# When the early weight conversions run in a fused retention, max-MLP and gated-MLP kernel

## The chip, the cores and the metric

The kernel runs on one core of one Trainium2 chip. The metric is the device time of one launch in microseconds (us). Three runs of the kernel before gave 906.43, 902.74 and 906.63 us; the median is 906.43 us.

## The reference

Three layers follow one another. The input has 4 sequences of 576 tokens, 8 heads of 64, so 2304 tokens of 512 features.

```python
scores = (1 / sqrt(64)) * q @ k.T                      # per batch and head
ret = (scores * D) @ v                                  # D[i, j] = gamma_h ** (i - j) for i >= j, else 0
x = ret as (2304, 512)
h = maximum(maximum(x @ w1, x @ w2), x @ w3)            # 512 -> 768   "first layer"
x = h @ w_out                                           # 768 -> 512   "second layer"
g = x @ w_gate; val = x @ w_val                         # 512 -> 1536  "third layer"
out = (g * sigmoid(g) * val) @ w_out2                   # 1536 -> 512
```

The weights arrive as 64-bit floats, seen by the kernel as pairs of 32-bit words.

## The kernel before, in words

**Precision.** Every product of matrices is made in three matmuls of a high and a low part (`xh`, `xl`, `wh`, `wl`). Each matmul has 288 columns (512 in the last product).

**Conversions and spills.** `conv32` turns one 128x512 tile of 64-bit weights into 32-bit floats: two ScalarE (ACT) instructions at L106 and L107, then three VectorE (DVE) instructions at L108 to L110. The 18 tiles of w1, w2, w3 are converted early and stay on the chip. The other 42 tiles are what this case is about: `spill()` loads one such tile (SP queue, 512 KB), converts it, and stores it to a scratch tensor `wd` in memory (SP queue, L298, 256 KB). The order of the 42 is fixed: six tiles of w_out, then, for each pair `k` = 0 to 5 of third-layer column groups, two of w_gate (`g`), two of w_val (`v`), two of w_out2 (`p`). Three buffers hold tiles that are loaded ahead.

**Stages.** The attention runs as 32 units `n` (a sequence, a half of 288 tokens, a pair of heads). From n = 4 on it is mixed with the first layer: after each unit come slices (`f_slice`, L311), one slice being 12 matmuls into one of two PSUM buffers, taken out by ACT (`hmax`, L315) or by a DVE maximum (L317), and stored to `h_d` after the third. After the last unit come the last 18 slices, mixed with the loads of the second layer's weights (`wo_load`, L377 to L380) and of its first inputs (`h_split`: load `hf` L387, high part `hh` on ACT L390, low part `hl` on POOL or DVE L391). The second layer is eight passes `o` (L470), each with four groups of 18 matmuls (L487), each group taken out by ACT (L492 in the first four passes, L496 in the last four). The inputs of pass `o + 1` are loaded and split during pass `o`. In passes 1 and 3 `x_ops` (L420 to L429) makes the third layer's inputs of the first half with a chain of DVE and ACT work; in passes 4 to 7 the result goes through memory (`x2d`, L502) for the second half. The third layer uses a seven-product scheme in place of eight (`half`, L577), with its weights prepared by `w_ops` (loads of `wd` into `sf` and `s`, DVE sums L456 to L459, ACT high parts L455 to L462, POOL low parts L460 to L465) and `p_ops` (load `of` L521, high part `ph` L523, low part `pl` on POOL L524).

**What sets the order.** TensorE (PE) follows the written order in the attention and in the third layer. Everything else is placed by a list scheduler that models the times of the instructions and issues an instruction as early as its model allows; the program that results is fixed, and each engine and the SP queue then run it strictly in that order, one waiting instruction holding all behind it. `paced` is the hook against too much earliness: the conversion of a spill is not placed before the instructions kept in `pace`. In the attention and the first layer these are the last `hmax` instructions. For the second layer `pace.clear()` (L469) empties it, so that the spills called there (L499) may be placed as early as the model likes.

**Where spills are called before.** One after each unit from n = 9 on (L359, 23 spills), one more where n is 12, 16, 20, 24, 28 (L363, 5), one in each of the six rounds of last slices (L398), one at the end of each of the eight passes of the second layer (L499).

Of the kernel before, what the change touches and what calls it, by code (L numbers as in the profile page):

```python
# [13 lines left out]
ACTF = mybir.ActivationFunctionType  # L14
# [13 lines left out]
NHB = 2 * B  # L28
# [34 lines left out]
def retention_moe(ctx, tc, consts, q, k, v, w1, w2, w3, w_out, w_gate, w_val, w_out2, out):  # L63
    nc = tc.nc
    pe, act, dve, pool, sp = nc.tensor, nc.scalar, nc.vector, nc.gpsimd, nc.sync
# [36 lines left out]
    def conv32(t):  # L102
        u = t.bitcast(U32).rearrange("p (n two) -> p n two", two=2)
        z = stg.tile([P, 512], U32, name="wz", tag="wz", bufs=2)
        l = stg.tile([P, 512], U32, name="wl", tag="wl")
        act.activation(f(z), f(u[:, :, 1]), ACTF.Copy, scale=float(2.0 ** -112))  # L106
        act.activation(l, u[:, :, 0], ACTF.Copy, scale=float(2.0 ** -29))  # L107
        dve.tensor_scalar(z, z, 3, None, ALU.logical_shift_left)  # L108
        dve.scalar_tensor_tensor(z, u[:, :, 1], 0x80000000, z, ALU.bitwise_and, ALU.bitwise_or)
        dve.tensor_tensor(l, z, l, ALU.add)  # L110
        return f(l)
# [16 lines left out]
    def a_load(n):  # L128
        if n >= NU:
            return  # L130
        b, h, pr = units[n]
        c0 = h * C
        u = {}
        for nm, s in (("k", k), ("q", q), ("v", v)):
            if nm == "q" and n >= PT:
                continue
            u[nm] = att.tile([CK, NC, 2, D], F32, name=f"{nm}n", tag=f"{nm}n", bufs=4)
            for e in range(2):
                sp.dma_start(out=u[nm][:, :, e, :],
                             in_=s[b, 2 * pr + e, c0:c0 + C].rearrange("(a p) d -> p a d", p=CK))  # L140
        if n >= PT:
            u["t"] = att.tile([P, 2, C // 32, 32], F32, name="qk", tag="qk", bufs=3)
            for i, s in enumerate((k, q)):
                for e in range(2):
                    for x in range(2):
                        g = 64 * e + 32 * x
                        sp.dma_start(out=u["t"][g:g + 32, i],
                                     in_=s[b, 2 * pr + e, c0:c0 + C, 32 * x:32 * x + 32].rearrange("(a p) d -> p a d", p=32))
        U[n] = u
# [71 lines left out]
    def a_value(n):  # L221
        b, h, pr = units[n]
        u = U.pop(n)
        z = stz[n % 3]
        o = psa.tile([P, C], F32, name="o_ps", tag="o_ps")
        for c in range(NC):
            for e in range(2):
                oc = o[64 * e:64 * e + 64, c * CK:(c + 1) * CK]
                if c or h:
                    pe.matmul(oc, z[:, c, e], u["qg"][:, c], start=c == 1 - h, stop=False, skip_group_check=True)  # L230
        for c in range(NC):
            for e in range(2):
                pe.matmul(o[64 * e:64 * e + 64, c * CK:(c + 1) * CK], u["v"][:, c, e], u["pT"][:, e, c],
                          start=False, stop=True, skip_group_check=True)
        xh, xl = [ffn.tile([P, C], F32R, name=f"x{x}", tag=f"x{x}{pr}", bufs=3) for x in "hl"]
        act.activation(xh, o, ACTF.Copy)
        dve.tensor_tensor(xl, o, f(xh), ALU.subtract)
        xs[(2 * b + h, pr)] = (xh, xl)
# [11 lines left out]
    def win_conv(i):  # L250
        if i >= len(win_units):
            return
        if i not in win_ld:
            win_load(i)
        win_load(i + 1)
        hi = ffn.tile([P, 512], F32R, name="wh", tag=f"wh{i}")
        lo = ffn.tile([P, 512], F32R, name="wlo", tag=f"wlo{i}")
        l = conv32(win_ld.pop(i))
        act.activation(hi, l, ACTF.Copy)
        pool.tensor_tensor(lo, l, f(hi), ALU.subtract)  # L260
        w_in[win_units[i]] = (hi, lo)
# [10 lines left out]
    pace = {}  # L272

    def paced(*names):

        st = ExitStack()
        for nm in names:
            if nm in pace:
                st.enter_context(tc.issue_after(pace[nm]))
        return st  # L280

    def sp_load(i):
        if i < len(sp_units) and i not in sp_ld:
            with paced("sp"):
                sp_ld[i] = load_w(sp_units[i][1])

    def spill():
        i = sp_n[0]
        if i >= len(sp_units):
            return  # L290
        sp_n[0] += 1
        sp_load(i)
        with paced("act", "dve"):
            l = conv32(sp_ld.pop(i))
        sp_load(i + 1)
        sp_load(i + 2)
        wd[sp_units[i][0]] = t = dram.tile([P, 512], F32, name=f"wd{i}", tag=f"wd{i}")
        sp.dma_start(out=t, in_=l)  # L298
# [3 lines left out]
    def f_slice(hb, fi, wi):  # L302
        wh, wl = w_in[(fi, wi)]
        cw = TOK[hb][1]
        ps = ps_mm.tile([P, C], F32, name="ps", tag="mm")[:, 0:cw]
        n = 0
        for kc in range(KD):
            xh, xl = xs[(hb, kc)]
            ksl = slice(kc * P, kc * P + P)
            for l, r in ((wh, xl), (wl, xh), (wh, xh)):  # L310
                pe.matmul(ps, l[:, ksl], r, start=n == 0, stop=n == 3 * KD - 1)  # L311
                n += 1
        if wi == 0:
            mx[hb] = ffn.tile([P, C], F32, name="hmax", tag="hmax", bufs=3)[:, 0:cw]
            pace["act"] = act.activation(mx[hb], ps, ACTF.Copy).ins  # L315
        else:
            pace["dve"] = dve.tensor_tensor(mx[hb], ps, mx[hb], ALU.max).ins  # L317
        if wi == 2:
            pace["sp"] = sp.dma_start(out=h_d[hb][fi], in_=mx[hb]).ins
# [3 lines left out]
    def f_some(n):  # L323
        for _ in range(n):
            if fq:
                f_slice(*fq.pop(0))
# [15 lines left out]
    for n in range(NU):  # L342
        if n % NP == 0 and n:
            fq += [(n // NP - 1, fi, wi) for fi in range(F1) for wi in range(3)]
        a_load(n + 4)
        a_value(n)
        a_state(n + 1)
        a_score(n + 1)
        quota, ncv = ((2, 3) if n >= 9 else (1, 2)), 0
        if 1 <= n < 4:  # L350
            ncv = 1
        elif 4 <= n < 9:
            ncv = 3
        for _ in range(min(ncv, len(win_units) - wc)):
            win_conv(wc)
            wc += 1
        f_some(quota[0])
        if n >= 9:
            spill()  # L359
        a_prep(n + 2)  # L360
        f_some(quota[1])
        if n >= 9 and n % 4 == 0:
            spill()  # L363
    pe_order.__exit__(None, None, None)
    psa_cm.__exit__(None, None, None)
# [29 lines left out]
    for i in range(F1):  # L395
        wo_load(i)
        h_split(0, i)
        spill()  # L398
        f_some(3)
    ffn_cm.__exit__(None, None, None)  # L400


# [11 lines left out]
    def x_tiles(blk):  # L414
        X[blk] = [xp.tile([P, 7, KH, C], F32R, name=f"x{x}", tag=f"xo{x}{blk}") for x in "hl"]
# [54 lines left out]
    for o in range(NHB):  # L470
        hb = order2[o]
        sb, blk, side = hb // 4, hb % 2, (hb // 2) % 2
        if sb == 0:
            if side == 0:
                x_tiles(blk)
                sc = [scratch() for j in range(KH)]
        else:
            st2 = wr.tile([P, 7, C], F32, name="sf", tag="sf")
        for e in (0, 2, 1, 3):
            ps = ps_mm.tile([P, C], F32, name="ps2", tag="mm")  # L480
            n = 0
            for fi in range(F1):
                wh, wl = wo[fi]
                hh, hl = hsp[(o, fi)]
                es = slice(e * P, e * P + P)
                for l, r in ((wh, hl), (wl, hh), (wh, hh)):
                    pe.matmul(ps, l[:, es], r, start=n == 0, stop=n == 3 * F1 - 1)  # L487
                    n += 1
            j, kh = e % KH, e // KH
            if sb == 0:  # L490
                sf, b12 = sc[j]
                act.activation(b12 if side and not kh else sf[:, 2 * side * kh + (1 - side) * kh], ps, ACTF.Copy)  # L492
                if side and kh:
                    x_ops(blk, j, sf, b12)
            else:
                act.activation(st2[:, e], ps, ACTF.Copy)  # L496
            for fi in ((0, 1), (3, 4), (2,), (5,))[e]:
                h_split(o + 1, fi)
        spill()  # L499
        if sb:  # L500
            x2d[hb] = t = dram.tile([P, KD, C], F32, name=f"x2d{hb}", tag=f"x2d{hb}")
            sp.dma_start(out=t, in_=st2[:, 0:KD])  # L502
            if o == NHB - 4:
                w_ops("g", 0)
            elif o == NHB - 3:
                w_ops("v", 0)
# [183 lines left out]
```

## Time and profile before

| quantity | value |
|---|---|
| median of three runs | 906.43 us (902.74 to 906.63) |
| the profiled execution's own time | 902.81 us |
| span of that execution's trace | 901.0 us |
| PE busy | 833.3 us, 92% of the span |
| DVE, ACT, POOL busy | 563.5, 395.0, 317.4 us |
| mean granted TensorE clock | 0.972 of full speed |

The span is the time from the first to the last instruction, 1.8 us less than the execution's own time. The work of PE is the same whatever the other engines do, so the time is read as PE's work plus PE's idle stretches plus what a lowered clock adds. In the profile's positions (us from the span's start) the attention with spills lies at about 98 to 326, the last slices at 326 to 361.4, the second layer at 361.4 to 459.7, and the third layer begins in earnest after that, a few of its products being mixed into the second layer's end.

### The profile page before, as it was taken

Reading aid. Unit: us, or ns where it says so; the run is one execution under the profiler, and the core shown is the slowest. Engines: PE = TensorE matmul, PEld = TensorE weight load, DVE = VectorE, ACT = ScalarE, POOL = GpSimd, SP = SyncE. Lnnn points to the kernel's source line nnn. Section 1 sums busy time; section 2 is a strip of 40 time slices with the busy share of each in tenths; the row PEclk is TensorE's granted clock in tenths of the full one; section 3 lists DMA queues with packets and bytes.
Section 4 is the critical chain, followed back from the end, with each engine's and each line's share of the span. In section 5 each row is a group of like instructions: output and inputs, shape, how many; then the busy total and the mean of one; then the engine's idle time right before and its main releaser. Section 6 shows DMA issues by size and latency. Waiting matters only on the chain.

```text
span 901.0 us, 17296 instructions
## 1 busy us (share of the span) xinstructions
PE 833.3 (92%) x6424; PEld 781.1 (87%) x6424; DVE 563.5 (63%) x1092; ACT 395.0 (44%) x916; POOL 317.4 (35%) x345
## 2 busy tenths in 40 slices
PE   6578899999999999879979999999998999999998
PEld 5477889999999999779879989998897998989997
DVE  3599556565565567646344575766798467567545
ACT  3465223233333345645456445344464554534431
POOL 3244100000010011133555564663656546546421
PEclk9589999999999999999999999999999999999999
DMA  7997676675766458833451210211134211120003
GB/s 167 211 215 190 163 182 156 162 197 150 195 165 168 145 185 271 276 91 111 139 164 36 64 48 25 66 43 35 53 120 130 67 53 48 27 62 18 1 2 105
DMA packets 170340, 105.99 MB, mean 118 GB/s; under 512 B 107664, under 2 KB 155792, under 8 KB 170256
## 3 DMA queue, kind: packets, MB, share of 16 engines
q1 hardware_dynamic: 170256, 104.89, 42.4%
q8 instruction: 50, 0.82, 0.4%
q14 instruction: 34, 0.28, 0.1%
HBM read 79.68 MB, written 25.17 MB: 116 GB/s over the span
## 4 chain that ended last, share of the span: by engine, by line
PE 38%; DVE 6%; DMA 3%; issue 2%; POOL 2%; ACT 2%; SPq 1%; DVEq 0%; POOLq 0%; ACTq 0%
PE ps L547 14%; PE g L570 12%; PE v L570 12%; DMA sf<-wd 2%; DVE sg L615 1%; DVE acc L553 1%; DVE t L632 1%; DVE sf L456 1%; PE ps L487 1%; POOL wl L463 1%; DVE sf L458 0%; DVE t L598 0%; DMA sf<-x2d 0%; DVE sf L459 0%; DMA hf<-h_d 0%
## 5 line engine op out<-in xcount | busy, mean ns | idle before, releaser
L311 PE MATMUL ps<-xl,wh 128*128 128x288 f32 x576 | 175.8, 305 | 16.6 <-ACT hmax L315 10.8
L311 PE MATMUL ps<-xh,wh 128*128 128x288 f32 x576 | 171.3, 297 | 0.0
L311 PE MATMUL ps<-xh,wlo 128*128 128x288 f32 x576 | 170.4, 296 | 0.0
L311 PEld LDWEIGHTS ps<-xl,wh 128*128 128x128 f32 x576 | 109.3, 190 | 23.4 <-ACT hmax L315 12.9
L311 PEld LDWEIGHTS ps<-xh,wlo 128*128 128x128 f32 x576 | 109.5, 190 | 0.0
L311 PEld LDWEIGHTS ps<-xh,wh 128*128 128x128 f32 x576 | 109.4, 190 | 0.0
L570 PE MATMUL g<-xl,wh 128*128 128x288 f32 x336 | 101.2, 301 | 4.8 <-DVE sg L615 2.0
L570 PE MATMUL v<-xl,wh 128*128 128x288 f32 x336 | 100.1, 298 | 1.1 <-DVE t L602 1.1
L570 PE MATMUL g<-xh,wl 128*128 128x288 f32 x336 | 100.4, 299 | 0.5 <-POOL wl L460 0.5
L570 PE MATMUL g<-xh,wh 128*128 128x288 f32 x336 | 100.0, 298 | 0.0
L570 PE MATMUL v<-xh,wl 128*128 128x288 f32 x336 | 99.7, 297 | 0.0
L570 PE MATMUL v<-xh,wh 128*128 128x288 f32 x336 | 99.6, 296 | 0.0
L160 POOL TENSOR_TENSOR ks<-kn,cst 96x384 f32<-96x384 f32 (+1 forms) x32 | 25.9, 809 | 198.7 <-PE m_ps L205 121.1
L641 POOL TENSOR_TENSOR gl<-t,gh 128x288 fp32r<-128x288 f32 (+1 forms) x72 | 55.1, 766 | 110.4 <-ACT gh L640 78.2
L553 DVE TENSOR_TENSOR acc<-ps,acc 128x512 f32<-128x512 f32 x90 | 61.9, 688 | 29.1 <-PE ps L547 29.0
L547 PE MATMUL ps<-ph,gl 128*128 128x512 f32 x192 | 76.1, 396 | 2.1 <-DVE acc L553 2.1
L547 PE MATMUL ps<-ph,gh 128*128 128x512 f32 x192 | 76.4, 398 | 0.0
L547 PE MATMUL ps<-pl,gh 128*128 128x512 f32 x192 | 75.6, 394 | 0.0
L317 DVE TENSOR_TENSOR hmax<-ps,hmax 128x288 f32<-128x288 f32 x96 | 43.1, 449 | 47.7 <-PE ps L311 23.3
L570 PEld LDWEIGHTS g<-xl,wh 128*128 128x128 f32 x336 | 64.3, 191 | 7.7 <-DVE sg L615 2.2
L487 PE MATMUL ps<-hl,woh 128*128 128x288 f32 x192 | 58.5, 305 | 11.5 <-ACT sf L492 5.0
L391 POOL TENSOR_TENSOR hl<-hf,hh 128x288 fp32r<-128x288 f32 x24 | 27.2, 1135 | 116.0 <-ACT hh L390 113.3
(113 smaller groups left out, 2035.1 us busy)
## 6 DMA issues: line engine op xcount, KB each, us to landing
wd<-wl SPq DMA_DIRECT2D x42, 256.0 KB, 3.6
w<-in_moe_w_dram SPq DMA_DIRECT2D x18, 512.0 KB, 4.8
w<-in_moe_w_out_dram SPq DMA_DIRECT2D x18, 512.0 KB, 4.8
h_d<-hmax SPq DMA_DIRECT2D x48, 144.0 KB, 2.0
hf<-h_d SPq DMA_DIRECT2D x48, 144.0 KB, 2.4
w<-in_moe_w_gate_dram SPq DMA_DIRECT2D x12, 512.0 KB, 5.1
w<-in_moe_w_val_dram SPq DMA_DIRECT2D x12, 512.0 KB, 5.2
sf<-wd SPq DMA_DIRECT2D x24, 256.0 KB, 3.1
```

Source lines behind the costliest of these rows:

```text
L160: pool.tensor_tensor(u["ks"][:, 0:nk], u["k"][:, 0:nk], sc, ALU.mult)
L311: pe.matmul(ps, l[:, ksl], r, start=n == 0, stop=n == 3 * KD - 1)
L317: pace["dve"] = dve.tensor_tensor(mx[hb], ps, mx[hb], ALU.max).ins
L391: (pool, dve)[fi % 2].tensor_tensor(hl, hf, f(hh), ALU.subtract)
L456: dve.tensor_tensor(q[4], a21, q[2], ALU.add)
L463: pool.tensor_tensor(lo[:, 4:6], sf[:, 4:6, 0:QW], f(hi[:, 4:6]), ALU.subtract)
L487: pe.matmul(ps, l[:, es], r, start=n == 0, stop=n == 3 * F1 - 1)
L547: pe.matmul(ps, l, r, start=n == 0, stop=n == 5)
L553: dve.tensor_tensor(acc[s], ps, acc[s], ALU.add)
L570: pe.matmul(bank, w[l][:, a, js], x[r][:, i, j], start=start and n == 0, stop=stop and n == 3 * KH - 1, skip_group_check=True)
L615: dve.tensor_tensor(t, c, t, ALU.mult)
L641: pool.tensor_tensor(gl, o[:, c0:c1], f(gh), ALU.subtract)
```

## The change

The 42 spills are called at other places. In the attention the second spill of a unit comes at every even n from 10 on, 11 units where there were 5. In the last slices only the first four of six rounds have a spill, and it is called after the slices of the round where it was called before them. In the second layer only the last four passes have one, and there the ACT instruction that takes out a group is now entered into `pace`, so that those four conversions are not placed before it. So 34, 4 and 4 spills stand where 28, 6 and 8 did. From L403 on the line numbers of the changed kernel move by 1 and later by 2.

```diff
-        if n >= 9 and n % 4 == 0:
+        if n >= 9 and n % 2 == 0:
             spill()
...
         h_split(0, i)
-        spill()
         f_some(3)
+        if i < 4:
+            spill()
...
             else:
-                act.activation(st2[:, e], ps, ACTF.Copy)
+                pace["act"] = act.activation(st2[:, e], ps, ACTF.Copy).ins
...
-        spill()
+        if o >= NHB - 4:
+            spill()
```

On ACT, where the first layer ends and the second begins (`hmax` takes out a slice, `sf<-ps` takes out a group of the second layer, `wz` and `wl` are the two conversion instructions), there stood before:

```order
L315 ACTIVATE hmax<-ps 128x288
L106 ACTIVATE wz<-w_4724 128x512
L107 ACTIVATE wl<-w_4724 128x512
L106 ACTIVATE wz<-w_4908 128x512
L106 ACTIVATE wz<-w_5055 128x512
L107 ACTIVATE wl<-w_4908 128x512
L107 ACTIVATE wl<-w_5055 128x512
L492 ACTIVATE sf<-ps_4785 128x288
L492 ACTIVATE sf<-ps_4817 128x288
L106 ACTIVATE wz<-w_5188 128x512
L107 ACTIVATE wl<-w_5188 128x512
L492 ACTIVATE sf<-ps_4843 128x288
```

and in the changed kernel:

```order
L315 ACTIVATE hmax<-ps 128x288
L106 ACTIVATE wz<-w_4566 128x512
L107 ACTIVATE wl<-w_4566 128x512
L315 ACTIVATE hmax<-ps 128x288 x2
L493 ACTIVATE sf<-ps_4829 128x288
L493 ACTIVATE sf<-ps_4861 128x288
L493 ACTIVATE sf<-ps_4887 128x288
L390 ACTIVATE hh<-hf 128x288 x3
L493 ACTIVATE sf<-ps_4919 128x288
L390 ACTIVATE hh<-hf 128x288 x3
```

All conversions that the scheduler had drawn into the second layer's first two passes are gone from there; the next one on ACT stands in pass 4.

On DVE, at the passage from the second layer to the third (`t<-g`, `t<-v` and `sg` are the first third-layer block's own work; `sf` with `s_6228` and with `s_6246` are the sums for the weights of k = 1 `v` and k = 2 `g`), there stood before:

```order
L459 TENSOR_TENSOR sf<-sf 128x256
L590 TENSOR_TENSOR t<-g_5916,t 128x288
L590 TENSOR_TENSOR t<-v_5945,t 128x288
L615 TENSOR_TENSOR sg<-t,sg 128x288
L632 TENSOR_TENSOR t<-t,sg 128x288
L598 TENSOR_TENSOR t<-g_5917,t 128x288
L598 TENSOR_TENSOR t<-v_5946,t 128x288
L615 TENSOR_TENSOR sg<-t,sg 128x288
L602 TENSOR_TENSOR t<-g_5915,t 128x288
L632 TENSOR_TENSOR t<-t,sg 128x288
L458 TENSOR_TENSOR sf<-sf,s_6228 128x256
L456 TENSOR_TENSOR sf<-s_6228,sf 128x256
```

and now:

```order
L460 TENSOR_TENSOR sf<-sf 128x256
L108 TENSOR_SCALAR wz<-wz 128x512
L109 SCALAR_TENSOR_TENSOR wz<-w_5611,wz 128x512
L110 ISA wl<-wz,wl 128x1024
L459 TENSOR_TENSOR sf<-sf,s_6228 128x256
L457 TENSOR_TENSOR sf<-s_6228,sf 128x256
L458 TENSOR_TENSOR sf<-sf 128x256
L460 TENSOR_TENSOR sf<-sf 128x256
L592 TENSOR_TENSOR t<-g_5916,t 128x288
L459 TENSOR_TENSOR sf<-sf,s_6246 128x256
L592 TENSOR_TENSOR t<-v_5945,t 128x288
L457 TENSOR_TENSOR sf<-s_6246,sf 128x256
```

The last spill's three instructions and the four sums for k = 1 `v` now stand ahead of the block's first `t`, and those for k = 2 `g` stand between its next ones.

On the SP queue at the same place (`x2d` and `wd<-wl` are stores, `sf`, `s` and `of` loads of prepared weights; the `of` loads feed `p_ops`), there stood before:

```order
L451 DMA s_6246<-wd_3505 128x256
L521 DMA of<-wd_2429 128x512
L502 DMA x2d_5853<-sf 128x1152
L521 DMA of<-wd_2573 128x512
L450 DMA sf<-wd_2919 128x2x256
L452 DMA sf<-wd_3009 128x256
L450 DMA sf<-wd_3442 128x2x256
L452 DMA sf<-wd_3505 128x256
L521 DMA of<-wd_3152 128x512
L521 DMA of<-wd_3298 128x512
```

and now:

```order
L504 DMA x2d_5853<-sf 128x1152
L451 DMA sf<-wd_2658 128x2x256
L453 DMA sf<-wd_2747 128x256
L298 DMA wd_5851<-wl 128x512
L451 DMA sf<-wd_3042 128x2x256
L453 DMA sf<-wd_3185 128x256
L452 DMA s_6637<-wd_3342 128x256
L523 DMA of<-wd_2296 128x512
L523 DMA of<-wd_2359 128x512
L452 DMA s_6655<-wd_3786 128x256
L523 DMA of<-wd_2889 128x512
L523 DMA of<-wd_2952 128x512
```

The first two `of` loads, which stood around the last `x2d` store, now come behind both `sf` pairs, the last spill's store and one `s` load; on ACT, too, all four `ph` now stand ahead of the `sg` that reads the product `g_5915`.

## Rows read from the trace of the kernel before

**Rows 1.** Windows: stretch, length, then busy (count) PE, PEld, DVE, ACT, POOL, PEclk, DMA.

```profile
98.00:326.00 228.00, 221.78 (x2241) 212.47 (x2240) 131.09 (x295) 70.78 (x164) 13.34 (x18) 1.00 0.64 167
326.00:361.40 35.40, 33.78 (x253) 33.09 (x252) 26.29 (x48) 18.58 (x39) 5.32 (x5) 1.00 0.83 270
361.40:402.00 40.60, 31.31 (x213) 29.78 (x213) 24.58 (x43) 22.11 (x46) 9.70 (x7) 0.96 0.57 186
402.00:424.60 22.60, 21.92 (x164) 21.46 (x162) 13.26 (x24) 13.25 (x29) 6.75 (x7) 1.00 0.38 110
424.60:459.70 35.10, 33.01 (x240) 31.90 (x239) 11.25 (x16) 12.69 (x30) 15.16 (x16) 1.00 0.41 131
459.70:477.00 17.30, 12.41 (x68) 11.93 (x69) 11.38 (x23) 11.12 (x27) 13.83 (x14) 0.80 0.63 194
```

**Rows 2.** Waits of PE from 361.4 to 402: total us, times, longest.

```profile
PE ps L487 <- ACT sf L492: 5.0, 3, 2.5
PE ps L487 <- POOL hl L391: 4.0, 2, 2.4
```

**Rows 3.** Timeline of ACT, 364 to 372: start, us, operation, idle before and releaser.

```profile
366.21 0.66 ACT L106 ACTIVATE wz<-w 128x512 f32<-128x512 f32 x1 [1.42 <-DMA w<-in_moe_w_gate_dram]
...
368.02 0.71 ACT L492 ACTIVATE sf<-ps 128x288 f32<-128x288 f32 x2
```

**Rows 4.** Timeline of PE at 396.

```profile
396.23 0.40 PE L487 MATMUL ps<-hl,woh 128*128 128x288 f32 x1 [2.49 <-ACT sf L492]
```

**Rows 5.** Timeline of POOL, 386 to 413, then of DVE, 386 to 392.

```profile
386.59 4.84 POOL L391 TENSOR_TENSOR hl<-hf,hh 128x288 fp32r<-128x288 f32 x1 [3.38 <-ACT hh L390]
394.12 0.79 POOL L391 TENSOR_TENSOR hl<-hf,hh 128x288 fp32r<-128x288 f32 x1 [2.69 <-ACT hh L390]
...
411.37 1.98 POOL L391 TENSOR_TENSOR hl<-hf,hh 128x288 fp32r<-128x288 f32 x1 [4.87 <-ACT hh L390]
385.52 0.75 DVE L429 TENSOR_TENSOR xl<-sf,xh 128x576 fp32r<-128x576 f32 x1
...
390.04 0.75 DVE L429 TENSOR_TENSOR xl<-sf,xh 128x576 fp32r<-128x576 f32 x1
```

**Rows 6.** Groups by line: count | busy us, mean ns | idle before, releasers.

```profile
L106 ACT ACTIVATE wz<-w 128x512 f32<-128x512 f32 x60 | 40.2, 670 | 32.4 <-DMA w<-in_moe_w_dram 14.9 <-DMA w<-in_moe_w_out_dram 10.4 <-DMA w<-in_moe_w_val_dram 4.4
L107 ACT ACTIVATE wl<-w 128x512 uint32<-128x512 uint32 x60 | 39.6, 663 | 0.7 <-DMA w<-in_moe_w_dram 0.6
...
L524 POOL TENSOR_TENSOR pl<-of,ph 128x512 fp32r<-128x512 f32 x24 | 32.3, 1364 | 3.9 <-ACT ph L523 2.9 <-POOL wl L464 0.9
...
L523 ACT ACTIVATE ph<-of 128x512 fp32r<-128x512 f32 x24 | 14.9, 629 | 5.3 <-PE ps L547 4.0 <-DMA of<-wd 1.0
```

**Rows 7.** Timeline of PE, 459 to 474.

```profile
461.52 0.40 PE L570 MATMUL g<-xl,wh 128*128 128x288 f32 x1 [1.84 <-ACT t L583]
...
473.05 0.61 PE L570 MATMUL g<-xl,wh 128*128 128x288 f32 x1 [1.99 <-DVE sg L615]
```

**Rows 8.** Timeline of ACT, 459 to 466.

```profile
461.06 0.41 ACT L583 ACTIVATE t<-g 128x288 f32<-128x288 f32 x1
...
464.03 0.39 ACT L595 ACTIVATE t<-g 128x288 f32<-128x288 f32 x1
```

**Rows 9.** Timeline of DVE, 461 to 470.

```profile
461.50 0.46 DVE L590 TENSOR_TENSOR t<-g,t 128x288 f32<-128x288 f32 x1 [1.65 <-ACT t L583]
...
468.84 0.41 DVE L458 TENSOR_TENSOR sf<-sf,s 128x256 f32<-128x256 f32 x1
```

**Rows 10.** Timeline of the SP queue, 463 to 470.

```profile
464.75 0.59 SPq L452 DMA_DIRECT2D sf<-wd  x1
```

**Rows 11.** Tile view of sf, loads issued from 464.1 to 465.2.

```profile
DMA to landing us min/median/max: 2.7/2.8/3.0
```

**Rows 12.** Tile view of sf, loads issued from 453.2 to 454.5.

```profile
DMA to landing us min/median/max: 3.5/4.0/4.5
```

**Rows 13.** The page, part 6: DMA issues, count, size of one, us to landing.

```profile
of<-wd SPq DMA_DIRECT2D x24, 256.0 KB, 2.8
```

## The prediction

> **What bounds the kernel now.** The first part of the profile gives PE 833.3 of 901.0 us busy, so I read first, by windows, where PE is not busy and where its clock is below full [rows 1]. The attention with its 28 spills loses 228.00 - 221.78 = 6.2 us, the last slices 1.6, the second layer's first passes (361.4 to 402) 40.60 - 31.31 = 9.3, the next stretch (402 to 424.6) 0.7, the late passes 2.1, the passage into the third layer 17.30 - 12.41 = 4.9. The clock is at full in all but two of these: 0.96 in the first passes, which adds 40.6 x 0.04 = 1.6 us, and 0.80 in the passage. The waits of PE in the first passes then say who was late: ACT taking out a group (5.0 us in three waits) and POOL making a low part (4.0 us in two) [rows 2]. What held ACT stands in its timeline: at 366.21 a conversion of a spill had waited 1.42 us for its load, and the two evictions that PE needed ran only at 368.02, behind two pairs of conversions [rows 3].
>
> **The change part by part.** A spill costs ACT 0.670 + 0.663 = 1.33 us in two instructions [rows 6], and DVE and SP their share.
>
> *First passes.* The order shows no conversion left there. The 9.3 us of idle and 1.6 us of lowered clock, 10.9 in all, should shrink to what the following stretch loses with the same kind of work, evictions and one whole set of `x_ops`, but no spill: 0.7 us [rows 1]. I take -10.2 us. The other end: only the waits that a conversion caused directly go, and the two last ones stay, 2.49 us at 396.23 [rows 4] and the longer of POOL's, 2.4 [rows 2], with their 1.6 us of clock; that leaves a gain of 10.2 - 6.5 = 3.7.
>
> These two waits have one root. POOL's low part at 386.59 took 4.84 us where one at 394.12 took 0.79, while DVE ran without a pause from 385.52 to 390.79; in the next set of `x_ops`, with gaps in DVE's work, the one at 411.37 took 1.98 [rows 5]. In the first set DVE was catching up behind the spills; without them it should be paced by PE as in the second set, and I let the long hold go.
>
> The Trainium skill speaks against that (SBUF — State Buffer, section Who interferes with whom): a VectorE instruction with two inputs in SBUF and a GpSimd instruction that reads SBUF exclude one another for the whole of an instruction, and the later one waits. All of `x_ops` on DVE is of that kind, and the change leaves it as it is, so by the rule alone the 4.84 us may come back. The trace agrees on the hold but shows 1.98 as well as 4.84 us for the same pair of works.
>
> *Last slices.* Two of six spills go; a third of 1.6 us is -0.5. Ends: nothing, and all of 1.6.
>
> *Attention.* Six spills come in, each a second one in a unit. Evictions stand behind them on ACT. The 28 there now go with 6.2 us of idle, 0.22 each at most, because PE has two PSUM buffers; six more are 6 x 0.22 = +1.3. The low end is nothing. If none were hidden, ACT's part would be 6 x 1.33 = +8.0. I take the row for the same work at the same place.
>
> *Late passes 4 to 6.* Three conversions now stand on ACT behind the last eviction of a pass and ahead of `hh` instructions, which wait for loads of `hf`. I price them as those in the attention, 3 x 0.22 = +0.7; ends nothing and 3 x 1.33 = 4.0.
>
> *The passage to the third layer.* Here the order changes most. I follow it on the positions of before.
> - ACT: the fourth conversion stands between the last eviction and the copies `t<-g`, so these move from 461.06 [rows 8] by 1.3. One more store ahead of the load of k = 1 `g`, which ACT needs just before, adds an estimated 0.5 (a 256 KB load lands after 2.8 [rows 13] and I let a fifth of that show). All 1.8 us come on top of the wait of 1.84 [rows 7].
> - DVE: the first `t` stood at 461.50, the first sum for k = 1 `v` at 468.84 [rows 9]. Now the sums come first and need their loads. The second of these was issued at 464.75 [rows 10] and lands within 2.9 (the middle of 2.8 and 3.0 [rows 11]), at 467.7, with the 0.5 at 468.2. The three sums that follow, 0.41 each, bring the first `t` to 469.5, 8.0 us later than before.
> - ACT again: its `sg` waits for that `t`, and behind it stands `ph`, which needs the first `of`. On SP this load now stands behind an `s` load whose buffer the second sum frees at 468.6; issued at 469.0, landed 2.8 later at 471.8, `ph` 0.63 done at 472.4. Only then comes the copy at L595, which was at 464.03 [rows 8], and PE cannot add its sixth product before.
> - The `of` loads have two buffers. The third and fourth wait until POOL has made the low parts of the first and second, 1.36 each [rows 6]: 473.8 and 475.2. The fourth lands at 478.0, its `ph` ends at 478.6. Behind it on ACT stand an `sg`, a `gh`, a short `gsh` and the `sg` that frees product A, at about the 0.4 of L595 [rows 8] some 1.5 us; DVE's multiplication adds 0.4. PE's next block, before at 473.05 [rows 7], begins at 480.5.
>
> The term is +7.4 us. PE's clock falls after the waits there as it does now (0.80 [rows 1]); since the chain and not PE sets 480.5, I add nothing for it. The low end is +1.8, ACT's part, if the rest is hidden; below that it cannot be, as the conversion stands ahead of the copies in any case. High end: three loads in the chain (`sf`, first `of`, fourth `of`) each take 4.5, the slowest of this stretch [rows 12], in place of 2.8: 7.4 + 5.1 = 12.5.
>
> *Beyond.* The order of PE, ACT and POOL from the second block on is the same, so nothing is added.
>
> Sum: -10.2 - 0.5 + 1.3 + 0.7 + 7.4 = -1.3 us. On the profiled execution, 902.81 us (its span of 901.0 and 1.8 around it), that is 901.5. That execution lies 3.6 below the median of 906.43, so on the median I say 905.1.
>
> **Rivals** (all on the median).
> - *The passage is hidden.* DVE's order looks worse than it is: loads land before the second layer ends, and only the 1.8 us show. For it: PE is busy 33.0 of 35.1 us in the late passes [rows 1], so what feeds it there keeps up. Against it: the `sf` buffer of k = 1 `v` is released by POOL's work on k = 1 `g`, which is itself late. Then -1.3 - 5.6 = -6.9, 899.5 us.
> - *The loads in the passage are slow* (the other side of no change). The four steps above hang on three loads in a row; at 4.5 us each they cost 5.1 more, net +3.8, 910.2 us, slower than before. It decides from about 3.3 us per load, where 3 x 0.5 eats the gain of 1.3. For it: the load of k = 1 `g` took 4.0 and 4.5 in this very stretch [rows 12]. Against it: 2.8 is the median of the `of` loads [rows 13], and fewer transfers are under way when these go.
> - *POOL stays held in the first passes.* DVE still runs `x_ops` in one piece, the long POOL instruction and both waits behind it remain, 6.5 us less gain: +5.2, 911.6 us. For it: all of `x_ops` is unchanged. Against it: the 1.98 at 411.37 [rows 5]. The page cited above would have it so.
> - *The attention does not hide six more.* With all of ACT's 8.0 us exposed the net is -1.3 + 6.7 = +5.4, 911.8 us. Against it: 28 of them go with 6.2 us in all.
>
> **How the numbers follow.** Half a per cent, 4.5 us, is about what a measurement of this kernel can tell from no change; the runs of before spread by 3.9. Chances: my forecast 0.45, the passage hidden 0.24, slow loads 0.13, POOL held 0.08, the attention 0.05, something else 0.05. Faster by over 0.5%: the hidden passage, most of it (0.22), the low wing of my forecast (0.05), a part of the rest (0.02): 0.29. Slower by over 0.5%: POOL held (0.06), the attention (0.05), the wing of slow loads (0.04), the rest (0.02): 0.17. Within: 0.54. The range runs from 898.5, a little under the hidden passage, to 911, between slow loads and POOL held; the upper bounds together would go further and are left out with the 2 in 10.
>
> **What would show it.** Right: in the 40 us from the second layer's start PE's idle falls from 9.3 to about 1 us and the clock stays at full; the low parts on POOL take under 2 us there. At the passage, DVE's first `t` comes after sums for k = 1 `v` that waited for `sf`, ACT's `ph` wait for `of`, and PE waits for ACT's L597 and then for DVE's L617, 7 us more in all. In the attention PE's idle grows by 1 to 2 us. Wrong: a passage that loses 5 us or less has the loads landing earlier than I take them; a first pass that still loses 4 or more has another cause than the spills.

## The result and the profile after

The changed kernel takes 908.37 us (median of 20 runs, 902.32 to 913.72) against 903.01 of the kernel before in the same runs (20, 896.43 to 909.32): a ratio of 1.0076, interval 1.0055 to 1.0098. It is slower, by more than the half per cent that counts as a difference. The prediction was 905.1 us and no difference, so the time lies in its range and the sign is wrong.

The profiled execution of the changed kernel took 910.4 us (span 908.3), 7.6 more than the one of before. These are its windows, at the stretches with the same work as in [rows 1], columns as there (PE, PEld, DVE, ACT, POOL, PEclk, DMA share) and with GB/s behind the DMA share: attention, last slices, first passes, middle passes, late passes, passage.

```profile
100.20:334.90 234.70, 223.83 (x2241) 214.22 (x2241) 139.26 (x312) 77.80 (x176) 13.96 (x18) 0.99 0.68 179
334.90:373.10 38.20, 34.93 (x251) 34.47 (x251) 21.57 (x41) 15.06 (x33) 4.64 (x5) 0.96 0.78 252
373.10:413.70 40.60, 40.60 (x307) 40.54 (x306) 22.19 (x38) 22.29 (x48) 8.79 (x10) 1.00 0.29 79
413.70:436.30 22.60, 20.49 (x148) 19.48 (x146) 14.27 (x18) 10.53 (x25) 10.99 (x10) 1.00 0.59 177
436.30:459.90 23.60, 22.41 (x162) 21.55 (x161) 12.52 (x16) 11.13 (x25) 9.21 (x9) 1.00 0.40 134
459.90:482.00 22.10, 10.14 (x51) 9.37 (x50) 14.36 (x26) 10.25 (x25) 11.61 (x12) 0.85 0.49 159
```

The first passes are now without a gap at full clock (40.60 busy of 40.60, 31.31 before). The attention has more gaps: 234.70 - 223.83 = 10.9 us idle against 6.2. The passage has 12.0 idle against 4.9 [rows 1].

To compare kernels, the table cuts each trace at the same work of PE, read from its timeline: *attention*, from unit 9's first product with `pT` to that of unit 31; *slices*, from there to the end of the first layer; *second layer*, its first to its last product; *passage*, from there to the first product with the last matrix (`ph`). Times in us; the brackets hold the number of conversions called in the attention / slices / second layer.

| kernel | attention | slices | second layer | passage |
|---|---|---|---|---|
| before (28/6/8) | 229.2 | 36.5 | 98.0 | 23.9 |
| changed (34/4/4) | 235.9 | 39.4 | 86.6 | 32.5 |
| difference | +6.7 | +2.9 | -11.4 | +8.6 |

The four differences add up to 6.8 of the 7.3 us between the spans. Ahead of unit 9, where the order is the same in both, the changed kernel's execution lost 2.2, and behind the passage it won 1.7.

The attention of the table as windows, before and then changed:

```profile
95.85:325.04 229.19, 222.97 (x2269) 213.61 (x2266) 132.66 (x300) 71.42 (x166) 14.29 (x20) 1.00 0.64 167
98.02:333.94 235.92, 225.05 (x2271) 215.40 (x2268) 140.00 (x316) 78.40 (x178) 14.91 (x20) 0.99 0.68 179
```

Of its 6.7 us, 4.65 are idle (10.87 against 6.22) and 2.1 are longer work of PE (225.05 against 222.97), at a granted clock of 0.99 instead of 1.00.

How a gap in the attention comes about can be read at one place of the changed kernel, from its timelines: DVE first, then ACT, PE and SP, columns as in [rows 3], `...` where rows are left out.

```profile
230.46 0.69 DVE L109 SCALAR_TENSOR_TENSOR wz<-w,wz 128x512 uint32<-128x512 uint32 x1
233.62 0.48 DVE L175 STREAM_TRANSPOSE qt<-qk 128x288 f32<-128x288 f32 x1 [2.48 <-DMA qk<-in_q_dram]
234.02 0.24 DVE L215 SCALAR_TENSOR_TENSOR st<-st,cst,m_ps 128x64 f32<-128x64 f32 x1
...
235.45 0.73 ACT L219 ACTIVATE stz<-st 64x192 f32<-64x192 f32 x2 [4.51 <-DVE st L215]
236.21 0.41 ACT L315 ACTIVATE hmax<-ps 128x288 f32<-128x288 f32 x1
...
236.67 0.40 PE L311 MATMUL ps<-xl,wh 128*128 128x288 f32 x1 [1.87 <-ACT hmax L315]
...
229.90 0.43 SPq L147 DMA_DIRECT2D qk<-in_q_dram  x1
```

The last piece of `qk` for a later unit went out at 229.90 and DVE stood 2.48 us for it. Behind that transpose stood the state update, ACT's `stz` waited for the update, the eviction `hmax` stood behind `stz`, and PE waited 1.87 us for the eviction. No conversion's arithmetic stands in this chain on ACT.

The passage is the predicted chain. Timelines of the changed kernel, PE, then DVE, then ACT, and last the one wait of PE before the change that [rows 7] leaves out:

```profile
463.14 0.61 PE L572 MATMUL g<-xl,wh 128*128 128x288 f32 x1 [3.19 <-ACT t L585]
...
473.20 0.61 PE L572 MATMUL g<-xl,wh 128*128 128x288 f32 x1 [5.29 <-ACT t L597]
...
481.76 0.40 PE L572 MATMUL g<-xl,wh 128*128 128x288 f32 x1 [3.49 <-DVE sg L617]
467.26 0.43 DVE L459 TENSOR_TENSOR sf<-sf,s 128x256 f32<-128x256 f32 x1 [1.74 <-DMA sf<-wd]
...
469.34 0.44 ACT L616 ACTIVATE sg<-t 128x288 f32<-128x288 f32 x1 [4.06 <-DVE t L592]
472.22 0.63 ACT L525 ACTIVATE ph<-of 128x512 fp32r<-128x512 f32 x1 [2.43 <-DMA of<-wd]
...
476.96 0.63 ACT L525 ACTIVATE ph<-of 128x512 fp32r<-128x512 f32 x1 [2.33 <-DMA of<-wd]
```
```profile
470.01 0.40 PE L570 MATMUL v<-xl,wh 128*128 128x288 f32 x1 [1.09 <-DVE t L602]
```

PE's three waits before were 1.84 (for `t<-g`), 1.09 and 1.99 (for `sg`); now they are 3.19, 5.29 and 3.49. DVE waits for the load ahead of its sums, ACT's `sg` waits 4.06 for the `t` behind them, and `ph` waits for `of`.

### The profile page after: what moved, and what is told of

It reads as the page before. It is cut to its first block, busy times and chain, and to the rows that moved or that the text cites. A ratio compares the mean times of both kernels' runs of the same rounds, so it can differ in the third digit from the quotient of the medians.

```text
span 908.3 us, 17274 instructions
## 1 busy us (share of the span) xinstructions
PE 836.4 (92%) x6424; PEld 785.2 (86%) x6424; DVE 568.7 (63%) x1092; ACT 395.0 (43%) x916; POOL 313.7 (35%) x345
## 5 line engine op out<-in xcount | busy, mean ns | idle before, releaser
L311 PE MATMUL ps<-xl,wh 128*128 128x288 f32 x576 | 178.0, 309 | 21.9 <-ACT hmax L315 13.9
L311 PE MATMUL ps<-xh,wh 128*128 128x288 f32 x576 | 173.4, 301 | 0.0
L311 PE MATMUL ps<-xh,wlo 128*128 128x288 f32 x576 | 172.5, 299 | 0.0
L311 PEld LDWEIGHTS ps<-xl,wh 128*128 128x128 f32 x576 | 111.4, 193 | 28.6 <-ACT hmax L315 16.1
L311 PEld LDWEIGHTS ps<-xh,wlo 128*128 128x128 f32 x576 | 111.7, 194 | 0.0
L311 PEld LDWEIGHTS ps<-xh,wh 128*128 128x128 f32 x576 | 111.3, 193 | 0.0
L572 PEld LDWEIGHTS g<-xh,wl 128*128 128x128 f32 x336 | 64.3, 191 | 3.0 <-POOL wl L461 0.9
L572 PEld LDWEIGHTS v<-xl,wh 128*128 128x128 f32 x336 | 64.0, 190 | 3.2 <-ACT wh L456 0.9
```

What stands on the lines that cost most here:

```text
L572: pe.matmul(bank, w[l][:, a, js], x[r][:, i, j], start=start and n == 0, stop=stop and n == 3 * KH - 1, skip_group_check=True)
```

## The experiments

The theory after the first comparison: the first passes and the passage are as predicted, and the attention pays several times what was forecast. The rivals on the attention's price are the conversions' arithmetic in front of the evictions, which is how the prediction priced it, and their transfers. The same table for all kernels follows, with the median of the runs and the ratio to the kernel before, run beside it (its medians were 901.8 to 902.2). The stages come from one profiled execution each:

| kernel | attention | slices | second layer | passage | median | ratio, interval |
|---|---|---|---|---|---|---|
| e1 late ones a pass earlier | 235.1 | 36.4 | 86.4 | 24.5 | 896.95 | 0.9928, 0.9897 to 0.9959 |
| e2 attention's part alone | 240.4 | 36.7 | 85.8 | 24.7 | 896.46 | 0.9946, 0.9909 to 0.9982 |
| e3 the six left out | 230.4 | 36.5 | 87.7 | 32.6 | 903.87 | 1.0004, 0.9976 to 1.0033 |
| e4 transfers of the six only | 234.4 | 38.4 | 87.7 | 32.6 | 905.47 | 1.0038, 1.0008 to 1.0069 |
| e5 arithmetic of the six only | 229.0 | 35.6 | 86.9 | 32.5 | 903.87 | 1.0013, 0.9981 to 1.0045 |
| e6 two in each of four passes | 233.1 | 37.6 | 93.4 | 24.8 | 897.35 | 0.9941, 0.9910 to 0.9971 |
| e7 spread | 231.4 | 37.1 | 85.8 | 22.4 | 891.19 | 0.9863, 0.9821 to 0.9905 |
| e8 changed kernel again | 239.1 | 37.2 | 88.3 | 33.4 | 910.94 (1 run) | |
| e9 loads of the six only | 230.3 | 36.8 | 86.8 | 31.2 | 903.75 | 1.0010, 0.9979 to 1.0041 |
| e10 stores of the six only | 232.9 | 37.2 | 87.6 | 33.1 | 904.43 | 1.0044, 1.0011 to 1.0077 |
| e11 q and k pieces earlier | 225.1 | 36.7 | 88.0 | 33.3 | 895.95 | 0.9949, 0.9923 to 0.9974 |
| e12 spread, pieces earlier | 222.1 | 37.1 | 87.1 | 23.3 | 884.56 | 0.9821, 0.9790 to 0.9851 |

The profiled execution is not always a middling one. In e5 and e9 it was the fastest of ten, in e3 the fastest but one (3.2, 6.8 and 2.9 us under their medians); in e2, e6, e7 and e12 it was the slowest (7.3, 4.9, 2.6 and 2.0 above). A few microseconds between two attentions can therefore belong to the executions; the ratios, from all the runs, carry more weight.

### e1: the late conversions one pass earlier

```diff
-        if o >= NHB - 4:
+        if NHB - 5 <= o < NHB - 1:
             spill()
```
(and line 493 sets `pace["act"]` as line 497 does)

> The changed kernel with its four late conversions in passes 3 to 6 of the second layer instead of 4 to 7 (pass 3's evictions set the pacing too). In the order of the instructions only one set of DVE's weight sums then stands ahead of the third layer's first t<-g, as in the kernel before. Theory A, the two sets of sums (and their loads) that stood ahead of it are what made the passage 22.1 us instead of 13.7: passage 13 to 15 us, time about 908.4 - 8 = 900.4 us. Rival B, the passage is long because the loads of the weights come late behind the conversions' traffic wherever these stand: passage over 18 us, time 904 to 908 us.

The passage is 8.0 us shorter than in the changed kernel's trace, at unchanged second layer. PE's waits in its timeline add up to 5.8 us, near the 4.9 of the kernel before; the first and the last of them:

```profile
457.52 0.40 PE L572 MATMUL g<-xl,wh 128*128 128x288 f32 x1 [1.59 <-ACT t L585]
...
469.12 0.61 PE L572 MATMUL g<-xl,wh 128*128 128x288 f32 x1 [1.58 <-DVE sg L617]
```

A holds: the passage's price was that of the one conversion in pass 7 and of the order it brought, not of late conversions as such. Up to the end of the slices every engine's order is that of the changed kernel, yet the slices took 36.4 and not 39.4.

### e2: the attention's part alone

```diff
-        if n >= 9 and n % 4 == 0:
+        if n >= 9 and n % 2 == 0:
```
(in the kernel before; the loop over the second layer then has two conversions left)

> The kernel before with the attention's part of the change alone: 34 conversions in the attention, six in the last slices as before, and two instead of eight in the second layer (passes 0 and 1). Theory A, the six more cost the attention 6.7 us by themselves: from unit 9 to unit 31 about 235.9 us (229.2 before), the last slices about 36 us as before if their own rearrangement cost the 2.9 us there, about 39 us if it is what the attention's traffic leaves late; time 903.0 + 6.7 and less whatever the second layer saves with two conversions instead of eight (0 to 10 us): 900 to 910 us. Rival B, the attention's 6.7 us came with the profiled execution and not with the conversions: 229 to 231 us from unit 9 to unit 31.

A's attention comes out, 240.4 us, but in an execution that was the slowest of the ten (902.0 of span). The median of 896.46 lies under the 900 to 910 that A expected: the second layer won 12.2 us, where at most 10 had been allowed for. This second layer is as short as any, with two unpaced conversions. Where they run fits that. ACT's timeline in this kernel, whose second layer begins at 376.12:

```profile
372.08 0.66 ACT L106 ACTIVATE wz<-w 128x512 f32<-128x512 f32 x1 [3.67 <-DMA w<-in_moe_w_out_dram]
...
375.04 0.67 ACT L106 ACTIVATE wz<-w 128x512 f32<-128x512 f32 x1 [1.44 <-DVE wl L110]
```

And in the kernel before, whose second layer begins at 361.37, the first and the last of seven:

```profile
362.66 0.67 ACT L106 ACTIVATE wz<-w 128x512 f32<-128x512 f32 x1 [4.58 <-DMA w<-in_moe_w_out_dram]
...
379.32 0.67 ACT L106 ACTIVATE wz<-w 128x512 f32<-128x512 f32 x1 [0.52 <-DVE wl L110]
```

Unpaced conversions are pulled forward. With two left, ACT is done with them as the layer begins; with eight, seven came in one heap over its first 18 us.

### e3, e4, e5: the six added conversions in parts

In all three the second spill of units 10, 14, 18, 22, 26 and 30 is replaced:

```diff
-        if n >= 9 and n % 2 == 0:
+        if n >= 9 and n % 4 == 0:
             spill()
+        elif n >= 9 and n % 2 == 0:
+            part_spill()
```
e3: `part_spill` does nothing. e4: it makes the load and the store (of a fixed tile). e5: it makes `conv32(fix)` on a tile loaded at the start. The later layers then read the scratch tile of the unit ahead (e3, e5) or zeros (e4) for these six weights; their own work stays the same.

> The changed kernel without the six added conversions of the attention: their loads, their arithmetic and their stores are left out, and the weights concerned are read from the scratch tile of the unit ahead of them, so all later work is as in the changed kernel. Theory A, they cost the attention 6.7 us: unit 9 to unit 31 in 229 to 231 us (235.9 in the changed kernel), time about 908.4 - 6.7 = 901.7 us, and below it by up to 2.9 us if the last slices' loss hangs on their traffic. Prediction's price: 1.3 us in the attention, time 907 us.

> The changed kernel in which the six added conversions of the attention keep their load from DRAM and their store (of a fixed tile), while their arithmetic on ScalarE and VectorE is left out (so these six weights are zero in the second and third layer). Theory A, the price is paid through the transfers: SP and the queues carry more, the q pieces land later, VectorE stands longer at its transposes with the evictions behind them: unit 9 to unit 31 in 234 to 238 us. Theory B, the price is the arithmetic in front of the evictions on ScalarE and VectorE: 229 to 232 us. Time 901 to 904 us by B, 906 to 909 us by A.

> The changed kernel in which the six added conversions of the attention keep their arithmetic, on a tile that was loaded once at the start, and have neither load nor store (the later layers read the scratch tile of the unit ahead of them). Theory A, the transfers are what costs: unit 9 to unit 31 in 229 to 232 us, time 901 to 904 us. Theory B, the arithmetic in front of the evictions costs: 234 to 238 us, time 906 to 909 us. Values between in both of these two kernels would say that each carries a part.

The same window of 230 us in the changed kernel, then in e3, e4 and e5 (columns as above):

```profile
98.00:328.00 230.00, 219.13 (x2219) 209.64 (x2214) 136.88 (x309) 76.76 (x175) 14.93 (x20) 0.99 0.69 179
```
```profile
98.00:328.00 230.00, 223.32 (x2251) 214.54 (x2249) 131.76 (x298) 71.13 (x165) 13.66 (x19) 0.99 0.63 164
```
```profile
98.00:328.00 230.00, 221.23 (x2203) 212.30 (x2201) 130.49 (x293) 70.12 (x162) 13.26 (x18) 0.99 0.70 182
```
```profile
98.00:328.00 230.00, 223.31 (x2286) 214.32 (x2283) 140.77 (x317) 78.52 (x179) 14.55 (x19) 1.00 0.64 164
```

Without the six (e3) PE idles 6.7 us and the attention takes 230.4. With their arithmetic alone (e5), DVE is busy 9.0 us and ACT 7.4 us longer than in e3, and PE loses nothing: 229.0. With their transfers alone (e4), DVE and ACT do no more than in e3, the DMA share rises from 0.63 to 0.70, PE idles 8.8, and the attention takes 234.4. The traces speak for theory A, that the transfers carry the price.

The whole times show less. The six together do cost: e3 (1.0004, up to 1.0033) lies clear of the changed kernel (1.0076, from 1.0055), by 0.0072 or 6.5 us. Their arithmetic alone is not this price, for e5 ends at 1.0045. The transfers alone (1.0038, 1.0008 to 1.0069) overlap with e3 and with the changed kernel, and the two parts, 0.0009 and 0.0034 over e3, make up 0.0043 of the 0.0072. How much the transfers cost by themselves, and how much only together with the arithmetic, is not shown.

### e6: all eight in passes 3 to 6

```diff
-        spill()
+        if NHB - 5 <= o < NHB - 1:
+            spill()
+            spill()
```
(in the kernel before; both evictions, L492 and L496, also set `pace["act"]`; attention and slices as before)

> All eight conversions of the second layer in its passes 3 to 6, two in each, paced behind the eviction; attention and last slices as in the kernel before. Theory A, the 11.4 us of the second layer are the first passes' stalls and come back without the attention's price, and the passage stays at 13 to 15 us since the order there is that of the kernel before: time 903.0 - 11.4 = 891.6 us, with at most 4 us more for eight instead of four in the late passes. Rival B, the second layer's gain came from there being four conversions and not from where they stand: time 897 to 903 us.

The time, 897.35 us, is 5 us won instead of 11, and lies at the edge of rival B's range. The stages show a part of each: the passage stays at 24.8 and the first 40.6 us of the layer are clean (PE idle 0.4, clock 1.00), as A has it; but two conversions at a time do not fit in the later passes, where PE idles 8.9 us, so their number counts as well. The largest wait of PE there, and DVE ahead of it:

```profile
434.89 0.42 DVE L108 TENSOR_SCALAR wz<-wz 128x512 uint32<-128x512 uint32 x1
...
436.16 1.52 DVE L108 TENSOR_SCALAR wz<-wz 128x512 uint32<-128x512 uint32 x1
437.60 1.32 DVE L110 CUSTOM_DVE_ANT_0 wl<-wz,wl 128x1024 uint16<-128x1024 uint16 x1
438.85 1.21 DVE L109 SCALAR_TENSOR_TENSOR wz<-w,wz 128x512 uint32<-128x512 uint32 x1
439.98 1.51 DVE L391 TENSOR_TENSOR hl<-hf,hh 128x288 fp32r<-128x288 f32 x1
441.55 0.61 PE L487 MATMUL ps<-hl,woh 128*128 128x288 f32 x1 [4.12 <-DVE hl L391]
```

The same instruction takes 0.42 and 1.52 us. POOL stands idle beside the first and makes low parts of weights beside the slow ones. Its own are stretched too, the second of these from 1.28 (at 428.05):

```profile
438.34 1.17 POOL L465 TENSOR_TENSOR wl<-sf,wh 128x256 fp32r<-128x256 f32 x1
439.47 1.71 POOL L463 TENSOR_TENSOR wl<-sf,wh 128x512 fp32r<-128x512 f32 x1
```

### e7: the parts that cost nothing, together

```diff
-        if n >= 9 and n % 4 == 0:
+        if n >= 9 and (n % 4 == 0 or n >= 26 and n % 2 == 0):
...
-        spill()
+        if o < 2 or NHB - 5 <= o < NHB - 1:
+            spill()
```
(against the kernel before; slices as there; only pass 3 and later set `pace["act"]`)

> The parts that cost nothing, put together: in the attention only two conversions more than in the kernel before, in units 26 and 30, where the changed kernel's units took no longer; six in the last slices as in the kernel before; two that run ahead of the second layer, as the two that were left there with the attention's part alone; and one in each of passes 3 to 6. Theory A, each part costs what it cost in the runs so far: second layer 86 us instead of 98.0, passage about 24.5 us to the first product of the last matrix (23.9 before), attention 229 to 233 us: 902.2 - 11.5 = about 890.7 us. Rival B, fewer conversions in the second layer are paid for elsewhere in any case: 896 us, as in the two kernels that were best so far.

891.19 us, half a microsecond from theory A's 890.7. Units 26 and 30, where the changed kernel had shown no longer unit, took 10.14 and 10.12 us, as in the kernel before.

### e8: the changed kernel again

> The changed kernel once more, for a second trace of it. If the 2.9 us of the last slices belong to the order of its instructions, they take about 39.4 us again; if they belong to the one execution, about 36.5 us, as in the kernel with the late conversions a pass earlier, whose instructions up to there stand in the same order. The attention's cost is of the order: 234 to 240 us from unit 9 to unit 31; passage 31 to 33 us to the first product of the last matrix.

Attention and passage repeat (239.1 and 33.4). The slices take 37.2. Three executions of one order give 39.4, 36.4 and 37.2: the 2.9 us belong to the execution. In the first trace PE waited 2.03 us behind one load of `wof` for which ACT stood 4.02; why it came late there was not settled.

### e9 and e10: loads or stores

In `part_spill` of e4 only the load is kept (e9), or only the store (e10).

> The changed kernel in which only the loads of the attention's six added conversions are kept (512 KB each); their arithmetic and their stores are left out, and the later layers read the scratch tile of the unit ahead of them. If the loads carry the transfers' price, unit 9 to unit 31 takes 233 to 236 us (234.4 with loads and stores, 230.4 with neither); if the stores carry it, 229 to 232 us.

> The changed kernel in which only the stores of the attention's six added conversions are kept (256 KB each, of a fixed tile, so six weights are zero later); their loads and arithmetic are left out. If the stores carry the transfers' price, unit 9 to unit 31 takes 233 to 236 us; if the loads carry it, 229 to 232 us.

With the loads alone the attention takes 230.3, but in the fastest of ten executions. With the stores alone it takes 232.9, between the two expectations and within what the order of before gives in two executions (229.2 in its own trace, 233.1 in e6). The times lean to the stores (1.0044 against 1.0010), with overlapping intervals. Which of the two it is stays open.

### e11 and e12: the pieces of q and k a unit earlier

```diff
+    def qk_load(n):
+        if PT <= n < NU:
...
+            u["t"] = att.tile([P, 2, C // 32, 32], F32, name="qk", tag="qk", bufs=4)
...
+        qk_load(n + 5)
         a_load(n + 4)
```
The issue also moves ahead of the k and v tiles of its round. e11 is the changed kernel with it, e12 is e7 with it.

> The changed kernel, all its conversions in place, with the transposed q and k pieces issued one unit earlier, ahead of the k and v tiles, into four buffers instead of three. Theory A, the added transfers cost because the q pieces land later and VectorE stands at its transposes with the evictions behind: its wait for the q pieces falls from 22 to 25 us to under 10 us, unit 9 to unit 31 takes 226 to 231 us (235 to 240 in the changed kernel), time about 908.4 - 7 = 901 us. Theory B, the transfers cost in another way (the conversions' own loads come late, SP stands at its stores): the wait for the q pieces may go, and the attention stays at 234 us or more, time 905 to 909 us.

> The fastest kernel so far (two conversions more in the attention, six in the slices, two ahead of the second layer, one in each of passes 3 to 6), with the q and k pieces issued one unit earlier as well. By theory A the stalls that the attention had before the change go too (about 6 us of PE's idle time in it): 891.2 - 4 = about 887 us, attention 224 to 228 us. By theory B 890 to 893 us.

Waits of DVE and of PE in the changed kernel from 98 to 328 (total, times, longest):

```profile
DVE qt L175 <- DMA qk<-in_q_dram: 23.0, 13, 3.3
PE ps L311 <- DVE hmax L317: 6.7, 6, 2.3
PE ps L311 <- ACT hmax L315: 4.1, 3, 1.9
```

The same in e11 (L181 is its transpose, L323 its `hmax`), and its window:

```profile
DVE qt L181 <- DMA qk<-in_q_dram: 0.3, 1, 0.3
PE ps L317 <- DVE hmax L323: 2.8, 3, 1.4
98.00:328.00 230.00, 227.16 (x2311) 219.16 (x2309) 144.65 (x321) 81.17 (x183) 16.02 (x20) 1.00 0.71 187
```

And the window of e12:

```profile
98.00:328.00 230.00, 228.91 (x2335) 221.18 (x2332) 141.55 (x316) 78.01 (x178) 15.65 (x20) 1.00 0.66 178
```

All transfers are there in e11 (DMA share 0.71) and DVE and ACT do more in the window than in any other kernel; yet with the wait for the pieces gone PE idles 2.8 us instead of 10.9. The time, 895.95, and the attention, 225.1, lie below what theory A gave: most of the stalls that the attention had before the change went as well. The changed kernel falls from 908.37 to 895.95 with its passage as bad as ever. e12, without the bad passage, takes 884.56 us, 1.8% under the kernel before and the fastest of all; its PE idles 1.1 us in the window, with 30 conversions in the attention.

This shows where the idle time comes from, not that the added conversions make the pieces late. DVE's own wait for the pieces did not grow: from unit 9 to unit 31 it is 23.2 us in the kernel before (one wait of 3.0 in it is put down to another load in the profile) and 23.0 in the changed one, and the pieces land in 2.9 and 3.0 us (medians). What grew is the part of it that reaches PE. Followed back from each gap of PE, to what released the instruction or to the one before it on its engine, the gaps that lead to a transpose waiting for its piece add up to 4.5 us in the kernel before and 6.2 in e6; to 8.3, 10.1, 6.9 and 7.8 in the changed order (its two traces, e1, e2); to 4.2 in e3, 4.0 in e5, 3.3 in e9, 5.6 in e4 and 5.8 in e10; and to nothing in e11 and e12. Nor is all of the price gone with the wait: e11, with four conversions more in the attention, still takes 3.0 us longer there than e12, in one execution each.

## Why the prediction was wrong, point by point

*The step that failed* is the attention's +1.3 (0.22 each of six). It measured +6.7 between the two profiled executions. Four executions of the changed order (changed kernel twice, e1, e2) give 235.1 to 240.4, mean 237.6, and two of the order of before (its own and e6) 229.2 and 233.1, mean 231.2: +6.4. In whole times the six cost 6.5 us (e3 against the changed kernel). I counted a conversion's 1.33 us on ACT ahead of the evictions, and wrote "DVE and SP their share" without working it out. The arithmetic alone is not the price (e5), and PE's idle time hangs on an instruction that the sum did not contain: DVE's transpose, which waits for the last q piece with more urgent work behind it (e11). The trace of before had this wait, 20.2 us in 14 times in the window of [rows 1], and I did not ask what it held up. Dividing the old idle by the old 28 conversions was no measure either: that idle was mostly this wait, for with the pieces earlier it falls from 6.2 to 1.1 us with 30 conversions in place (e12). What in a further conversion lets more of the wait reach PE, its transfers alone or these with its arithmetic, stays open. The sign named beforehand, PE's idle growing by 1 to 2 us there, failed too: it grew by 4.65.

*The nearness of the time* is partly luck. The 905.1 us stood on 906.43 for the kernel before, the median of three runs; twenty give 903.01. Between the two kernels the forecast was -1.3 and the measured difference is +5.4, a miss of 6.7 us.

*The bound of 8.0* for the attention contained the result, by the wrong mechanism. The rival "does not hide six more" put it at 911.8 us with a chance of 0.05; the attention's 6.4 came near its 8.0, but its reason, ACT's arithmetic exposed, is not what e5 shows.

*First and late passes*: forecast -10.2 and +0.7, together -9.5; measured -11.4, and -9.7 in e8. The idle of the first passes is 0 and the clock at 1.00, where I had left 0.7 us. The late passes, from 413.7 to 459.9, idle 3.3 us against 2.8 in the two stretches that answer to them [rows 1]: +0.5. POOL's long hold did go. The low part made beside the first set of `x_ops` took 1.28 us, where it had taken 4.84 [rows 5]:

```profile
396.74 1.28 POOL L391 TENSOR_TENSOR hl<-hf,hh 128x288 fp32r<-128x288 f32 x1 [0.66 <-ACT hh L390]
```

My reason for it does not hold, though: DVE was to have gaps in its work, and it ran this set from 388.12 to 398.3 without a pause (the 0.66 above is POOL's). Three low parts on POOL fell into that time, the one above, which lost 0.5, and two that took 0.92 and 0.87. Why one of before lost 4 us was not settled.

The Trainium skill's rule (SBUF — State Buffer, Who interferes with whom) would have let the 4.84 come back, and it did not. In e6 the same rule fits: a VectorE instruction with two SBUF inputs, or a `tensor_scalar` in a two-port mode, and a GpSimd instruction that reads SBUF exclude one another, and the later one waits. DVE's L108, a `tensor_scalar`, took 1.52 there beside POOL's work and 0.42 without it. So the rule fits there; whether this `tensor_scalar` ran in such a mode no trace shows. It gives no price: the same kind of low part lost 4.0 us in one place and 0.1 to 0.5 in another.

*Last slices*: forecast -0.5, measured +2.9 in the one trace, but -0.1 and +0.7 in two more executions of that order (e1, e8). No steady gain, and no steady loss shown.

*The passage*: forecast +7.4, measured 22.10 instead of 13.67 us from the last product of the second layer to the block that had begun at 473.05 [rows 7], +8.4. The steps came out nearly in place, on positions shifted by 0.3: the load for the second sum landed at 467.50 (468.2 forecast, of which 0.5 was for one store more that did not show), the copy at L597 came after `ph` at 472.8 (472.4), the block at 481.76 (480.5). The loads of `of` landed in 2.6 to 4.0 us, median 2.8, so neither the hidden passage nor the slow loads came true. What I put too low is the end: beside POOL's low parts DVE's `sg` product took 1.29 us in place of 0.46.

With the attention at 6.4, the passage at 8.4 and the second layer at -11.4 the sum is +3.4 us, and +6.3 with the slices of the profiled execution; measured is +5.4 between the medians.

## What to carry to other kernels

A conversion that is "hidden" has three prices, arithmetic, loads and stores, and each must be set against the engine or queue that already waits in that stage, not against the busiest one. Look first for an instruction that waits for a DMA with more urgent work behind it on an in-order engine: moving that load ahead took 12.4 us off the changed kernel and 6.6 off e7, where the best placement of the conversions (e7) took 11 off the kernel before. And place late work by what stands behind it on each queue: one conversion in the last pass cost 8 us, the same one a pass earlier nothing.

## What the runs showed of the chip

One order of instructions gave an attention of 235.1, 235.9, 239.1 and 240.4 us in four executions. Part of it is the clock. In e2 and e8 a wait of PE of 3.00 and 2.73 us at one place in unit 14 made the unit 16.07 and 14.72 us long, where it takes 10.2 to 11.2: behind that wait PE ran at half clock, 1.2 GHz. So it did in the changed kernel's first trace behind the wait of 1.87 us shown above. Windows of e2 and of the changed kernel (length, PE busy, PEclk, DMA share, GB/s):

```profile
163.70:167.00 3.30, 3.30 (x14) 0.50 0.40 77
```
```profile
237.50:240.50 3.00, 3.00 (x14) 0.50 0.78 168
```

So one late transfer can cost more than its wait.
